# Attention in plain float32, with the second head mixing in two row tiles of TensorE

## The chip, the cores and the metric

The kernel runs on one core of a Trainium2 chip. The metric is the time of one execution on the device in microseconds (us). A core has engines that run side by side, each in its own order: TensorE (PE; its weight loads are listed as PEld), VectorE (DVE), ScalarE (ACT), GpSimd (POOL) and SyncE (SP), which here only issues DMAs. "Granted clock" is the share of TensorE's full 2.4 GHz that the chip gave it; the other level is 1.2 GHz.

## The reference

Attention with two mixings of its twelve heads, and then a mixture of eight experts, each token going to one.

```python
batch, n_heads, seq, head_dim = (8, 12, 448, 64)

scores = scale * np.matmul(q, k.transpose(0, 1, 3, 2))
scores = np.einsum('bhij,hg->bgij', scores, w_pre)          # first mixing of heads
scores = scores - np.max(scores, axis=-1, keepdims=True)
attn = np.exp(scores)
attn = attn / (np.sum(attn, axis=-1, keepdims=True) + 1e-09)
attn = np.einsum('bhij,hg->bgij', attn, w_post)             # second mixing of heads
attn_out = np.matmul(attn, v)
x = attn_out.transpose(0, 2, 1, 3).reshape(B * S, H * D)    # 3584 x 768
...
expert_idx = np.argmax(x @ w_gate, axis=1)                  # E = 8, D = 768, F = 1024
for e in range(E):
    h = np.maximum(x[expert_idx == e] @ w1[e], 0.0)
    out[expert_idx == e] = gate_w * (h @ w2[e])
```

## The kernel before, in words

Each batch has four tiles of queries, three of 120 and one of 88 (`it` 0 to 3; 32 tiles T). For a tile, `qk` computes the scores of one head: the keys and queries are split into a high and a low part in float32r (`ka` and `kb`, `qs`), stacked on the 128 partitions, and two matmuls over 448 keys add up in a PSUM bank `bs`. ScalarE copies it into `si` (queries on partitions, heads and keys along them). `relayout`, a DMA from SBUF to SBUF, turns blocks of 10 queries into `sb`, with the 120 pairs (query, head) on the partitions. `split` makes `sh` and `sl` of it on VectorE. `mix` is the first mixing: three float32r matmuls by the block matrix of `w_pre` (`WH`, `WL`) into a bank `bm`, a maximum on VectorE, the exponential on ScalarE into `et`, with its sum, and `wp`, the block matrix of `w_post` divided by the sums. `post` is the second mixing, which also transposes: for each of four chunks of 112 keys, `et` is the stationary operand (120 rows, 112 columns) and `wp` is streamed (120 columns) into a bank `bp`, which ScalarE copies into `pt`. `av` multiplies by the values `vt`, two heads at once in the two column halves of the array (64 columns each) into `ba`. `rows` turns the result into rows of x with the logits of the gate (`bx`), and `dispatch` sorts the tile's tokens to the experts. All plain float32 matmuls appear in the trace as two instructions each, each with its weight load; a float32r matmul appears as one.

The blocks of all tiles form one sequence of 360 steps u. A table, filled by `at(step, key, function, ...)`, says at which step each function is written, and within a step they are written in the order of their keys; a scheduler then orders each engine's instructions from that, staying close to it. In step u stand the `mix` of block u, the scores of a head of a tile to come (17 steps ahead of it), a relayout 5 steps ahead, a split 2 steps ahead, av of the tile before, and `post` of the block three steps back. The keys of the next batch are loaded and split while the scores of the last tile of a batch (`it == 3`) run, a chunk of two heads at a time through two buffers `kraw`; `vt` has one buffer, loaded after the last `av` of a batch. Behind the attention comes the stage of the experts (`turn_x`, `hidden`, `result`), which runs over the eight experts; its first weights (`load_w`) are loaded in the last steps of the attention.

Of the kernel before, what the change touches and what calls it, by code (L numbers as in the profile page):

```python
# [28 lines left out]
KC = 2                # heads of one chunk of keys  # L29
CAP = 512             # tokens per expert in the straight path  # L30
# [8 lines left out]
def attn_moe_kernel(ctx, tc, qT, kT, v, w_pre, w_post, w_gate, w1, w2, out):  # L39
# [5 lines left out]
    XD = dram.tile([NT, HD], F32, name="XD")          # rows of x by token  # L45
    TB = dram.tile([ROWS, 2], F32, name="TB")         # token id (int32) and gate of each expert's rows

    geom = []
    for T in range(NTILE):
        it = T % 4  # L50
        ni = min(IT, S - it * IT)
        geom.append((T // 4, it, ni, [min(IB, ni - s) for s in range(0, ni, IB)]))

# [1 line left out]
    kq = ctx.enter_context(ExitStack())  # L55
    kraw_p = kq.enter_context(tc.tile_pool(name="kraw", bufs=2, side="right"))
    k_p = kq.enter_context(tc.tile_pool(name="kp", bufs=6, side="right"))
    q_p = kq.enter_context(tc.tile_pool(name="qp", bufs=1, side="right"))
    att = ctx.enter_context(ExitStack())
    v_p = att.enter_context(tc.tile_pool(name="vp", bufs=1))  # L60
    si_p = att.enter_context(tc.tile_pool(name="sip", bufs=2))
    sb_p = att.enter_context(tc.tile_pool(name="sbp", bufs=4))
    sh_p = att.enter_context(tc.tile_pool(name="shp", bufs=3))
    e_p = att.enter_context(tc.tile_pool(name="ep", bufs=5))
    sm_p = att.enter_context(tc.tile_pool(name="smp", bufs=4))
    ps_s = att.enter_context(tc.tile_pool(name="ps_s", bufs=1, space=PSUM))
# [5 lines left out]
    bank_s = [ps_s.tile([P, 512], F32, name=f"bs{n}") for n in range(2)]  # L72
    bank_m = [ps_m.tile([IT, 512], F32, name=f"bm{n}") for n in range(2)]
    bank_p = [ps_p.tile([JC, 512], F32, name=f"bp{n}") for n in range(2)]
    bank_a = ps_a.tile([P, 3, IT], F32, name="ba")
    bank_x = [ps_x.tile([P, 512], F32, name="bx"), bank_s[0]]
    turn = {"s": 0, "m": 0, "p": 0}

    def bank(k, banks):
        turn[k] += 1  # L80
        return banks[turn[k] % len(banks)]

    KK, QQ, VV, SI, SB, SH, EE, PT, XT, KR = ({} for _ in range(10))

    def dma_k(b, c, pool):
        raw = pool.tile([P, KC, S], F32, name="kraw")
        src = kT[b, c * KC:(c + 1) * KC].rearrange("h d j -> d h j")
        for half in range(2):
            nc.sync.dma_start(out=raw[half * D:(half + 1) * D], in_=src)
# [582 lines left out]
```

## Time and profile before

| | us |
|---|---|
| median of 3 runs | 1741.92 |
| lowest and highest run | 1730.40 and 1745.09 |
| profiled execution: span from its first instruction to its last | 1726.5 |
| its own time beside the span | not recorded apart; the runs lie 3.9 to 18.6 above the span, the median 15.4 |

In the profiled execution TensorE is busy for 89% of the span, its weight loads for 78%, VectorE for 61%, ScalarE for 52% and GpSimd for 6%. These are averages over two stages of different kind: the attention, up to about 1150 us, and the experts. The end of a matmul is modelled by the profiler, so the pace of a group is read from its starts, or from its busy time less one instruction's duration.

### The profile page before, as it was taken

What the parts mean: (1) busy time and instruction counts of PE and PEld (TensorE: products, weight loads), DVE (VectorE), ACT (ScalarE), POOL (GpSimd) and SP (SyncE); (2) the same over time, 40 slices, a digit from 0 to 9 for tenths busy, and PEclk for the clock granted to TensorE, in tenths of its full rate; (3) what the DMA queues carried; (4) which work ended last, traced back from release to release, by engine and by line L of the source; (5) the groups of instructions that cost most, each with busy time, mean ns of one, the idle gap of its engine ahead of it and who ended that gap; (6) DMA issues with size and microseconds to landing.
All of it is one profiled execution on the core that took longest, in us unless ns stands there. A gap on an engine that the chain in (4) does not pass through costs nothing. (4 is left out here: it accounts for less than half of the span.)

```text
span 1726.5 us, 30276 instructions
## 1 busy us (share of the span) xinstructions
PE 1541.7 (89%) x11032; PEld 1341.1 (78%) x11032; DVE 1055.8 (61%) x3159; ACT 903.9 (52%) x1940; POOL 109.3 (6%) x119
## 2 busy tenths in 40 slices
PE   5878978987988988998898898968999999999996
PEld 3667867876876877786787787758898988898986
DVE  4677857876877777786786787753433425335330
ACT  4566756765766656675775676633422314224220
POOL 1000000000000000000000000010110201101000
PEclk9999988999999989998998999988999999999998
DMA  8666656666556666665665655634514326145210
GB/s 180 129 134 129 127 117 137 116 134 140 118 126 148 121 137 128 130 126 129 134 117 128 133 110 114 154 70 162 195 67 165 142 78 215 66 153 210 74 62 34
DMA packets 112169, 219.58 MB, mean 127 GB/s; under 512 B 28226, under 2 KB 83538, under 8 KB 112004
## 3 DMA queue, kind: packets, MB, share of 16 engines
q1 hardware_dynamic: 104896, 193.53, 48.3%
q0 software_dynamic: 6064, 23.86, 3.7%
q8 instruction: 98, 1.61, 0.4%
q14 instruction: 67, 0.55, 0.1%
q10 hardware_dynamic: 1044, 0.04, 0.0%
HBM read 118.03 MB, written 23.06 MB: 82 GB/s over the span
## 5 line engine op out<-in xcount | busy, mean ns | idle before, releaser
L256 PE MATMUL bp<-wp,et 120*112 120x120 f32 (+1 forms) x2880 | 386.1, 276 | 4.2 <-ACT pt L258 2.7
L256 PEld LDWEIGHTS bp<-wp,et 120*112 120x112 f32 (+1 forms) x2880 | 346.7, 180 | 45.4 <-issue 21.4
L258 ACT COPY pt<-bp 112x480 f32<-112x480 f32 x360 | 204.3, 568 | 143.1 <-PE bp L256 142.2
L208 ACT COPY si<-bs 120x448 f32<-120x448 f32 (+1 forms) x380 | 200.8, 531 | 140.4 <-PE bs L204 108.0
L271 PE MATMUL ba<-pt,vt 112*64 112x120 f32 (+1 forms) x3072 | 210.7, 276 | 50.1 <-DMA vt<-in_v 40.7
L237 ACT ACTIVATE et<-bm,st 120x448 f32<-120x448 f32 x360 | 229.5, 638 | 43.2 <-DVE st L235 34.9
L271 PEld LDWEIGHTS ba<-pt,vt 112*64 112x64 f32 x3072 | 162.6, 142 | 110.7 <-issue 95.5
L235 DVE TENSOR_REDUCE st<-bm 120x1 f32<-120x448 f32 x360 | 220.9, 614 | 12.4 <-PE bm L233 12.1
L224 DVE TENSOR_TENSOR sl<-sb,sh 120x448 fp32r<-120x448 f32 x360 | 220.5, 615 | 0.3
L223 DVE CAST sh<-sb 120x448 fp32r<-120x448 f32 x360 | 140.0, 389 | 101.6 <-PE bm L232 51.3
L203 PE MATMUL bs<-ka,qs 128*120 128x448 f32 (+1 forms) x384 | 153.7, 400 | 48.0 <-ACT si L208 33.1
L231 PE MATMUL bm<-sh,WH 120*120 120x448 f32 x360 | 167.6, 465 | 7.6 <-DVE sh L223 4.7
L204 PE MATMUL bs<-kb,qs 128*120 128x448 f32 (+1 forms) x384 | 148.5, 387 | 0.6 <-DVE kb L97 0.6
L500 PE MATMUL pm_h<-xh,ah 128*128 128x512 f32 (+1 forms) x384 | 146.9, 383 | 2.2 <-PEq L552 0.8
L500 PE MATMUL pm_h<-xl,ah 128*128 128x512 f32 (+1 forms) x384 | 146.4, 381 | 0.0
L500 PE MATMUL pm_h<-xh,al 128*128 128x512 f32 (+1 forms) x384 | 146.4, 381 | 0.0
L233 PE MATMUL bm<-sl,WH 120*120 120x448 f32 x360 | 137.6, 382 | 0.2 <-DVE sl L224 0.2
L232 PE MATMUL bm<-sh,WL 120*120 120x448 f32 x360 | 137.5, 382 | 0.0
L519 PE MATMUL pm_y<-bh,hh 128*128 128x384 f32 x480 | 127.9, 343 | 0.0
L504 DVE SCALAR_TENSOR_TENSOR hl<-pm_h,hh 128x512 fp32r<-128x512 f32 (+1 forms) x64 | 42.0, 656 | 136.3 <-ACT hh L503 136.3
L203 PEld LDWEIGHTS bs<-ka,qs 128*120 128x120 f32 (+1 forms) x384 | 72.6, 189 | 67.0 <-ACT si L208 39.9
L519 PE MATMUL pm_y<-bl,hh 128*128 128x384 f32 x480 | 123.6, 336 | 0.0
(106 smaller groups left out, 2177.4 us busy)
## 6 DMA issues: line engine op xcount, KB each, us to landing
sb<-si SPq DMA_DIRECT2D x352, 210.0 KB
wraw<-in_w SPq DMA_DIRECT2D x48, 512.0 KB
wraw<-in_w SPq DMA_DIRECT2D x64, 384.0 KB
kraw<-in_kT SPq DMA_DIRECT2D x96, 224.0 KB
qraw<-in_qT SPq DMA_DIRECT2D x48, 360.0 KB
vt<-in_v SPq DMA_DIRECT2D x8, 1344.0 KB
XD<-xr SPq DMA_DIRECT2D x24, 360.0 KB
qraw<-in_qT SPq DMA_DIRECT2D x16, 264.0 KB
```

The costliest lines, as they stand in the source:

```text
L203: nc.tensor.matmul(out=ps[:ni, :S], lhsT=qs, rhs=ka[:, h % KC, :], start=True, stop=False)
L204: nc.tensor.matmul(out=ps[:ni, :S], lhsT=qs, rhs=kb[:, h % KC, :], start=False, stop=True)
L208: nc.scalar.copy(out=SI[T][:ni, h, :], in_=ps[:ni, :S])
L224: nc.vector.tensor_sub(out=sl[:R], in0=sb[:R], in1=sh[:R].bitcast(F32))
L231: nc.tensor.matmul(out=pm[:R, :S], lhsT=WH[:R, :R], rhs=sh[:R], start=True, stop=False)
L235: nc.vector.reduce_max(out=st[:R, 0:1], in_=pm[:R, :S], axis=AX.X, negate=True)
L237: nc.scalar.activation(out=et[:R], in_=pm[:R, :S], func=AF.Exp, bias=st[:R, 0:1], scale=1.0, accum_out=st[:R, 1:2])
L256: nc.tensor.matmul(out=ppv[:, c, :], lhsT=et[:R, c * JC:(c + 1) * JC], rhs=wp[:R, :, :nb], start=True, stop=True)
L258: nc.scalar.copy(out=PT[T][:, :, :, s * IB:s * IB + nb].rearrange("p c h i -> p (c h) i"), in_=pp[:, :NJ * R].rearrange("p (x i) -> p x i" ...
L271: nc.tensor.matmul(out=pa[r * D:(r + 1) * D, :ni], lhsT=VV[b][:, c, h * D:(h + 1) * D], rhs=PT[T][:, c, h, :ni], start=(c == 0), stop=(c = ...
L500: nc.tensor.matmul(out=ph[:, :n], lhsT=wx[:, fs], rhs=xx[:, kt, :n], start=(m == 0), stop=(m == 3 * NK1 - 1))
L519: nc.tensor.matmul(out=py[g][:, :384], lhsT=hx[:, kt, ts], rhs=wx[:, g * 384:(g + 1) * 384], start=(n == 0), stop=(n == 3 * NK2 - 1))
```

## The change

The attention works on plain float32, without high and low parts. `qk` takes a pair of heads: the 64 features of one head lie on partitions 0 to 63, those of the other on 64 to 127, and each head's matmul uses only its row half of the array (64 rows), for 224 keys at a time, each head into its own bank of `bs`; one ScalarE copy takes both. The unit of a step is now 20 queries in two halves of 10 (NB = 2 * IB), 184 units in all. `mix` is one float32 matmul per half, with rows 4 to 123 in use (R0, R1), one maximum over both halves, two exponentials; `wp` is computed by GpSimd. In `post` the rows 4 to 63 hold 5 queries and the rows 64 to 123 the other 5, so that the block matrix has 60 columns (IQ = 5, WPC = 60) and each half of the rows is a matmul of its own, 64 and 60 rows, into its own bank (`bank_p[0]`, `bank_p[1]`); VectorE copies both into `pt`. `bs` and `bm` have a single buffer of two banks each. Keys have buffers for two batches and are loaded while the scores of the second tile (`it == 1`) run, each key once; `vt` has two buffers and is loaded at the eighth unit of the batch before. `post` runs one unit after `mix`, the scores up to 8 units ahead, the relayout 2 units ahead. The opening in which the first tile's scores were ordered by hand is gone.

```diff
+NB = 2 * IB
+IQ = 5
+WPC = H * IQ
+R0, R1 = 4, 124
...
+    bank_s = ps_s.tile([P, 2, 512], F32, name="bs")
+    bank_m = ps_m.tile([P, 2, 512], F32, name="bm")
...
+    def load_k(b, c):
+        kt = k_p.tile([P, S], F32, name="kt")
+        nc.sync.dma_start(out=kt, in_=kT[b, 2 * c:2 * c + 2].rearrange("h d j -> (h d) j"))
+        KK[b, c] = kt
...
+        for n in range(2):
+            ns = slice(n * S // 2, (n + 1) * S // 2)
+            for r in range(2):
+                hs = slice(r * D, (r + 1) * D)
+                nc.tensor.matmul(out=bank_s[:ni, r, ns], lhsT=qt[hs, c, :ni], rhs=kt[hs, ns],
+                                 start=True, stop=True)
+        nc.scalar.copy(out=SI[T][:ni, 2 * c:2 * c + 2, :], in_=bank_s[:ni, :, :S])
+        if it == 1 and b + 1 < B:
+            load_k(b + 1, c)
...
-        nc.tensor.matmul(out=pm[:R, :S], lhsT=WH[:R, :R], rhs=sh[:R], start=True, stop=False)
-        nc.tensor.matmul(out=pm[:R, :S], lhsT=WL[:R, :R], rhs=sh[:R], start=False, stop=False)
-        nc.tensor.matmul(out=pm[:R, :S], lhsT=WH[:R, :R], rhs=sl[:R], start=False, stop=True)
...
+        for c in range(nh):
+            nc.tensor.matmul(out=bank_m[:R1, c, :S], lhsT=Wpre[:R1, :], rhs=sb[:R1, c, :],
+                             start=True, stop=True)
+        nc.vector.reduce_max(out=st[:R1, 0, :nh], in_=bank_m[:R1, :nh, :S], axis=AX.X, negate=True)
+        for c in range(nh):
+            nc.scalar.activation(out=et[:R1, c, :], in_=bank_m[:R1, c, :S], func=AF.Exp,
+                                 bias=st[:R1, 0, c:c + 1], scale=1.0,
+                                 accum_out=st[:R1, 1, c:c + 1])
...
+        wp = e_p.tile([P, 2, WPC], F32, name="wp")
+        for c in range(nh):
+            nc.gpsimd.tensor_scalar(out=wp[:R1, c, :], in0=Wpost[:R1], scalar1=st[:R1, 2, c:c + 1],
+                                    scalar2=None, op0=ALU.mult)
...
-        for c in range(NJ):
-            nc.tensor.matmul(out=ppv[:, c, :], lhsT=et[:R, c * JC:(c + 1) * JC],
-                             rhs=wp[:R, :, :nb], start=True, stop=True)
-        nc.scalar.copy(out=PT[T][:, :, :, s * IB:s * IB + nb].rearrange("p c h i -> p (c h) i"),
-                       in_=pp[:, :NJ * R].rearrange("p (x i) -> p x i", i=nb))
...
+                for r in range(2):
+                    ps = slice(64 * r, 64 if r == 0 else R1)
+                    x0 = (n * NJ + c) * WPC
+                    nc.tensor.matmul(out=bank_p[r][:, x0:x0 + WPC],
+                                     lhsT=et[ps, n, c * JC:(c + 1) * JC],
+                                     rhs=wp[ps, n, :], start=True, stop=True)
...
+                nc.vector.tensor_copy(out=dst, in_=pv.rearrange("p n x i -> p x n i"))
...
-        if pr == NPAIR - 1 and it == 3 and b + 1 < B:
-            load_v(b + 1)
...
-    PL, QLEAD, RLEAD, SLEAD = 3, 17, 5, 2
+    PL, QLEAD, RLEAD = 1, 8, 2
...
+        if it == 0 and b + 1 < B:
+            at(u0 + 8, 2, load_v, b + 1)
+        for c in range(NPAIR):
+            at(max(u0 - QLEAD + c * 5 // 6, -1), 3, qk, T, c)
```

On TensorE, in the middle of the attention, a step before (L231 to L233 mixing, L203 and L204 scores, L271 av, L256 post, L289 rows; the numbers behind a row are how many matmuls in a row it stands for):

```order
L289 MATMUL bx<-xg,xt 120x136 x3
L231 MATMUL bm_106<-sh,WH 120x448
L232 MATMUL bm_106<-sh,WL 120x448
L233 MATMUL bm_106<-sl,WH 120x448
L203 MATMUL bs_104<-ka,qs 120x448
L204 MATMUL bs_104<-kb,qs 120x448
L271 MATMUL ba<-pt,vt 64x120 x8
L256 MATMUL bp_109<-wp,et 112x120 x4
```

And a unit after, at the same place (L209 mixing, L185 scores, L263 av, L237 post, L279 rows):

```order
L237 MATMUL bp_110<-wp,et 112x60
L279 MATMUL bx<-xg,xt 120x136 x3
L209 MATMUL bm<-sb_154,Wpre 124x448 x2
L185 MATMUL bs<-kt,qt 120x224 x4
L263 MATMUL ba<-pt,vt 64x120 x16
L237 MATMUL bp_109<-wp,et 112x60
L237 MATMUL bp_110<-wp,et 112x60
```

The order of the parts is the same; a unit holds two halves of the mixing in a row, a pair of heads, av of one or two pairs, and post as sixteen matmuls that change between the two banks.

On ScalarE where the keys of the next batch are loaded, before (L237 exponential, L258 copy of post, L208 copy of scores, L96 and L116 the high parts of keys and queries):

```order
L237 ACTIVATE et,st<-bm_106,st 120x448
L258 COPY pt<-bp_109 112x48x10
L96 CAST ka<-kraw 128x896
L237 ACTIVATE et,st<-bm_107,st 120x448
L208 COPY si<-bs_104 88x448
L116 CAST qs<-qraw 128x1440
```

And after (L213 exponential, L187 copy of scores, L281 copy of x, L311 exponential of the gate):

```order
L213 ACTIVATE et,st<-bm,st 124x448 x2
L187 COPY si<-bs 120x896
L281 COPY xr<-bx 120x384
L311 ACTIVATE ex,sc<-lgs,sc 120x8
L213 ACTIVATE et,st<-bm,st 124x448 x2
L187 COPY si<-bs 120x896
```

The casts that stood between the exponentials, and the copies of post, are gone from this engine.

On SP's queue at a change of batch, before (L215 relayout, L127 values, L296 rows of x, L109 queries, L89 keys):

```order
L215 DMA sb<-si 120x1x448 x4
L127 DMA vt<-in_v 112x4x768
L296 DMA XD<-xr 88x768
L215 DMA sb<-si 120x1x448 x7
L109 DMA qraw<-in_qT 64x1440
L215 DMA sb<-si 120x1x448
```

And after, at the values' place (L200 relayout, L101 values, L286 rows of x, L96 queries, L88 keys):

```order
L200 DMA sb_154<-si 120x1x448 x2
L101 DMA vt<-in_v 112x4x768
L200 DMA sb_151<-si 120x1x448 x2
L286 DMA XD<-xr 88x768
L200 DMA sb_152<-si 120x1x448 x2
L96 DMA qt<-in_qT 64x6x120
L200 DMA sb_153<-si 120x1x448 x2
```

The values are still issued among the relayouts, but these are now the values of the next batch.

## Rows read from the trace of the kernel before

**Rows 1.** Busy time of each engine in three stretches (before the first mixing, from the first to the last mixing, and after it); the columns are the stretch, its length, busy us and instructions of PE, PEld, DVE, ACT and POOL, the granted clock, the DMA engines' busy share, and GB/s.

```profile
0.00:31.90 31.90, 14.30 (x32) 7.96 (x32) 13.72 (x21) 15.31 (x22) 4.71 (x25) 0.93 0.88 197
31.90:1137.20 1105.30, 984.50 (x8051) 837.74 (x8052) 830.99 (x2798) 713.88 (x1640) 31.53 (x30) 0.94 0.61 128
1137.20:1726.50 589.30, 542.88 (x2952) 495.35 (x2950) 211.07 (x342) 174.74 (x279) 73.03 (x64) 0.97 0.35 122
```

**Rows 2.** The same columns, for an undisturbed stretch and two at a change of batch.

```profile
597.00:634.00 37.00, 37.00 (x330) 32.56 (x329) 30.41 (x106) 25.78 (x62) 0.99 (x1) 1.00 0.58 114
634.70:646.30 11.60, 5.09 (x35) 4.19 (x33) 5.13 (x30) 3.42 (x11) 0.63 (x1) 0.67 0.65 195
...
670.40:678.40 8.00, 3.51 (x23) 3.15 (x21) 3.63 (x10) 3.63 (x9) 0.00 (x0) 0.86 0.58 118
```

**Rows 3.** Waits over the whole span: who waited for whom, us in total, times, the longest.

```profile
ACT ka L96 <- DMA kraw<-in_kT: 55.7, 18, 7.0
DVE kb L97 <- ACT ka L96: 53.7, 25, 5.5
...
PE ba L271 <- DMA vt<-in_v: 40.7, 7, 6.8
...
PE bs L203 <- ACT si L208: 33.1, 14, 5.6
PE bx L289 <- DVE xt L275: 28.3, 7, 5.6
```

**Rows 4.** TensorE's instructions in order of time, a step with av at 88 queries and one without: start, busy us, engine, line, operation, tiles, rows and columns of the weights, what is streamed, and count.

```profile
608.13 0.45 PE L231 MATMUL bm<-sh,WH 120*120 120x448 f32 x1
608.41 0.37 PE L232 MATMUL bm<-sh,WL 120*120 120x448 f32 x1
...
609.02 0.37 PE L204 MATMUL bs<-kb,qs 128*120 128x448 f32 x1
609.32 0.83 PE L271 MATMUL ba<-pt,vt 112*64 112x88 f32 x16
610.08 1.07 PE L256 MATMUL bp<-wp,et 120*112 120x120 f32 x8
610.92 0.44 PE L231 MATMUL bm<-sh,WH 120*120 120x448 f32 x1
...
612.02 0.98 PE L256 MATMUL bp<-wp,et 120*112 120x120 f32 x8
612.76 0.45 PE L231 MATMUL bm<-sh,WH 120*120 120x448 f32 x1
```

**Rows 5.** TensorE's groups by line and shape, 597 to 634 us: busy us, mean duration of one instruction in ns, idle before.

```profile
L256 PE MATMUL bp<-wp,et 120*112 120x120 f32 x113 | 15.1, 273 | 0.0
...
L271 PE MATMUL ba<-pt,vt 112*64 112x88 f32 x96 | 5.0, 245 | 0.0
...
L256 PE MATMUL bp<-wp,et 96*112 96x96 f32 x8 | 0.9, 259 | 0.0
L289 PE MATMUL bx<-xg,xt 128*120 128x136 f32 x6 | 0.9, 279 | 0.0
```

**Rows 6.** As rows 4, for a group of rows and a post of 8 queries (96 columns).

```profile
602.80 0.86 PE L289 MATMUL bx<-xg,xt 128*120 128x136 f32 x6
...
604.50 0.93 PE L256 MATMUL bp<-wp,et 96*112 96x96 f32 x8
```

**Rows 7.** DMA issues by tile and size: engine, count, KB each.

```profile
kraw<-in_kT SPq DMA_DIRECT2D x96, 224.0 KB
qraw<-in_qT SPq DMA_DIRECT2D x48, 360.0 KB
vt<-in_v SPq DMA_DIRECT2D x8, 1344.0 KB
```

**Rows 8.** Groups of ScalarE and VectorE over the whole span, from the page: busy us, mean ns, idle before and what ended it.

```profile
L258 ACT COPY pt<-bp 112x480 f32<-112x480 f32 x360 | 204.3, 568 | 143.1 <-PE bp L256 142.2
L208 ACT COPY si<-bs 120x448 f32<-120x448 f32 (+1 forms) x380 | 200.8, 531 | 140.4 <-PE bs L204 108.0
...
L237 ACT ACTIVATE et<-bm,st 120x448 f32<-120x448 f32 x360 | 229.5, 638 | 43.2 <-DVE st L235 34.9
...
L235 DVE TENSOR_REDUCE st<-bm 120x1 f32<-120x448 f32 x360 | 220.9, 614 | 12.4 <-PE bm L233 12.1
```

**Rows 9.** GpSimd's copies of 128 columns, by line: busy us, mean ns.

```profile
L171 POOL COPY xg<-ident 128x128 f32<-128x128 f32 x6 | 1.5, 283 | 0.0
```

**Rows 10.** The last mixing in order of time: its last matmul, the maximum, and two exponentials in a row (in brackets the idle time before, and what ended it).

```profile
1137.69 0.37 PE L233 MATMUL bm<-sl,WH 96*96 96x448 f32 x1
...
1138.10 0.62 DVE L235 TENSOR_REDUCE st<-bm 96x1 f32<-96x448 f32 x1 [0.20 <-PE bm L233]
...
1138.97 0.64 ACT L237 ACTIVATE et<-bm,st 120x448 f32<-120x448 f32 x1
...
1139.59 0.63 ACT L237 ACTIVATE et<-bm,st 96x448 f32<-96x448 f32 x1
```

**Rows 11.** TensorE's first instruction, and its first mixing.

```profile
10.71 0.73 PE L203 MATMUL bs<-ka,qs 128*120 128x448 f32 x1 [10.71 <-ACT ka L96]
...
31.91 0.73 PE L231 MATMUL bm<-sh,WH 120*120 120x448 f32 x1
```

More of the change, by code (lines that the diff above doesn't have):

```diff
@@ L26 @@
 IB = 10
+NB = 2 * IB
+IQ = 5
+WPC = H * IQ
+R0, R1 = 4, 124
 JC, NJ = 112, 4
 NPAIR = H // 2
-KC = 2
 CAP = 512
@@ L77, in attn_moe_kernel @@
[L77 to L87, printed above, removed]
-        for half in range(2):
-            nc.sync.dma_start(out=raw[half * D:(half + 1) * D], in_=src)
-        KR[b, c] = raw
-    def split_k(b, c, eng=None):
-        raw = KR.pop((b, c))
-        ka = k_p.tile([P, KC, S], F32R, name="ka")
-        kb = k_p.tile([P, KC, S], F32R, name="kb")
-        nc.scalar.copy(out=ka, in_=raw)
-        (eng or nc.vector).tensor_sub(out=kb, in0=raw, in1=ka.bitcast(F32))
-        KK[b, c] = (ka, kb)
@@ L121, in load_q @@
-    def load_q(T):
-        dma_q(T)
-        split_q(T)
+    bank_x = [ps_x.tile([P, 512], F32, name="bx"), bank_s[:, 0, :]]
+    KK, QQ, VV, SI, SB, EE, PT, XT = ({} for _ in range(8))
+    def load_k(b, c):
+        kt = k_p.tile([P, S], F32, name="kt")
+        nc.sync.dma_start(out=kt, in_=kT[b, 2 * c:2 * c + 2].rearrange("h d j -> (h d) j"))
+        KK[b, c] = kt
+    def load_q(T):
+        b, it, ni, _ = geom[T]
+        qt = q_p.tile([P, NPAIR, IT], F32, name="qt")
+        src = qT[b, :, H * it * IT:H * (it * IT + ni)].rearrange("d (c t i) -> t d c i", c=NPAIR, t=2)
+        for half in range(2):
+            nc.sync.dma_start(out=qt[half * D:(half + 1) * D, :, :ni], in_=src[half])
+        QQ[T] = qt
@@ L135, in attn_moe_kernel @@
     nc.scalar.activation(out=warm, in_=warm, func=AF.Exp)
-    first = ExitStack()
-    first_p = first.enter_context(tc.tile_pool(name="kfirst", bufs=H // KC))
-    dma_q(0)
-    for c in range(H // KC):
-        dma_k(0, c, first_p)
+    load_q(0)
+    for c in range(NPAIR):
+        load_k(0, c)
     ident = const.tile([P, P], F32, name="ident")
     make_identity(nc, ident)
-    mask = const.tile([IT, IB], F32, name="mask")
+    mask = const.tile([P, IB], F32, name="mask")
     nc.gpsimd.memset(mask, 1.0)
@@ L168, in attn_moe_kernel @@
+    nc.vector.tensor_tensor(out=Wpost, in0=w12[:, 1, :].unsqueeze(2).to_broadcast([P, H, IQ]),
+                            in1=mask5.unsqueeze(1).to_broadcast([P, H, IQ]), op=ALU.mult)
+    Wpost = Wpost.rearrange("p g i -> p (g i)")
+    sbs = [sb_p.tile([P, 2, S], F32, name=f"sb{n}") for n in range(4)]
+    for t in sbs:
+        nc.gpsimd.memset(t, 0.0)
     xg = const.tile([P, NPAIR, XG], F32, name="xg")
@@ L249, in post @@
-        R = nb * H
         if s == 0:
@@ L392, in attn_moe_kernel @@
         at(ua + 5 * w // NPAIR + 2, 9, dispatch, T)
-    with tc.manual_schedule():
-        split_q(0)
-        split_k(0, 0)
-        split_k(0, 1)
-        for c in range(H // KC):
-            if c + 2 < H // KC:
-                split_k(0, c + 2)
-            for h in range(KC * c, KC * c + KC):
-                qk(0, h)
-    first.close()
-    pt_p = att.enter_context(tc.tile_pool(name="ptp", bufs=2))
-    x_p = att.enter_context(tc.tile_pool(name="xp", bufs=1))
     at(0, 2, load_v, 0)
```

154 lines of the change are left out of this document (61 added, 93 removed).

## The prediction

> **What bounds the kernel now.** I read the stretches first. Before the first head mixing lie 31.9 us, the mixing stage takes 1105.3 us, and from the last mixing to the end 589.3 us pass [rows 1]. The change rewrites the first two and leaves the experts alone. In the mixing stage TensorE is busy for 984.5 of 1105.3 us at a granted clock of 0.94, while VectorE has 831 us and ScalarE 714 us. So TensorE is the bound there, but not a clean one. In an undisturbed stretch it has no idle time and a clock of 1.00; where a batch changes, it is busy for 5.09 of 11.6 us (clock 0.67) and 3.51 of 8.0 us [rows 2]. The waits name the causes: 40.7 us for vt (one buffer, asked for when the last batch is done with it), and 33.1 and 28.3 us for ScalarE's and VectorE's copies, which stand in line behind casts and subtractions of keys whose DMA is late (55.7 and 53.7 us) [rows 3].
>
> To price the undisturbed part I went to TensorE's order of time. A step without av, from one L231 to the next, takes 612.76 - 610.92 = 1.84 us; one with av at 88 queries 610.92 - 608.13 = 2.79 us [rows 4]. Paces come from the same rows. float32r with 448 columns: 609.02 - 608.41 for three, 0.203 us each. A float32 matmul shows as two instructions, each with its own weight load. At 120 columns a group of eight takes 0.98 us, less one duration 0.273 [rows 4, 5], over 7: 0.101 us each; at 136 columns (0.86 - 0.279)/5 = 0.116 [rows 5, 6]. That is 0.85 ns per column. At 96 columns it should be 0.082 and is (0.93 - 0.259)/7 = 0.096: there something else sets the pace, and what is left is the load of 112 weight columns. The av group, in two column halves, does 16 instructions of 88 columns in 0.83 us: (0.83 - 0.245)/7 = 0.083 us per pair, where two in a row would need 0.15. So halves of the array do overlap, and their loads with them (this is columns, not rows). The step with av is 0.95 us longer, its 8 pairs are 0.66: 0.29 us for going into and out of the split mode, 0.145 per switch.
>
> Before, by these paces: mixing 1080 x 0.204 = 220, scores 768 x 0.204 = 157, post 2880 x 0.101 = 291, av 162 (below), rows 384 x 0.116 = 45, switches 384 x 0.145 = 56; 931 us. The stage took 1105: 174 us are lost. Idle time is 1105.3 - 984.5 = 121, and a clock of 0.94 means that 12% of the time ran at 1.2 GHz, which costs some 66 [rows 1]; the two explain it.
>
> **The change, part by part, on TensorE.**
> Scores: per pair of heads four float32 matmuls of 224 columns, eight instructions of 224 x 0.85 = 0.190 us. If both row halves run at once, four pairs in a row: 0.76 us; 32 tiles x 6 pairs x 0.76 = 146 us (before 157). The halved contraction buys no time: it pays for float32.
> First mixing: 360 halves x 2 instructions x 448 x 0.85 ns (0.381 us) = 274 us. That is dearer than three float32r passes (220).
> Post: per ten queries four chunks, two row halves, two instructions: 16 instead of 8, with 60 columns. Matmuls at 60 columns would need 0.051 us, but each loads 112 weight columns, 0.096 us [rows 5, 6]. With both halves loading at once 360 x 8 x 0.096 = 276 us (before 291): the row tiles halve the streaming, and the load takes its place. Bounds: 147 us if a load of 64 rows hides entirely (pairs at 0.051), 553 us if the two halves load one after the other. I take 276, since the only split groups in the trace, av's, load in pairs.
> The rows have no load with fewer than 96 rows. The Trainium skill, TensorE: Matmul & The Clock Gate, section LDWEIGHTS (loading the stationary operand), says that a load takes the columns divided by 1.2 GHz, whatever the rows; for 112 columns that gives an estimate of 93 ns, near this trace's 96, and it speaks against the hope in row tiles: with it post would come to about 269 us, and not to 147.
> av is unchanged: 48 pairs per tile, 0.083 us at 88 queries, 0.113 at 120 (by columns): 24 x 48 x 0.113 + 8 x 48 x 0.083 = 162 us. Rows: 45 us.
> Switches: mixing uses the whole array, scores and post row halves, av column halves. A unit of 20 queries with all four has four switches where two steps had two on average; over a tile's six units I count 21, some 650 in all: 94 us at 0.145. Between zero and twice that: 0 to 188.
> The rows show this cost for column halves only. The Trainium skill, TensorEngine Tiling (Array Packing), Key Properties, says that any change of tiling mode drains the engine; if instead only column mode cost, the total would fall by some 39 us.
> Sum: 146 + 274 + 276 + 162 + 45 + 94 = 997 us of work for the stage, 66 us **more** than before; 5.4 us for each of the 184 units.
>
> **What goes away.** The losses. Keys lose cast and subtraction and land as they are, in twelve buffers, asked for a tile of queries earlier; vt has two buffers and is asked for at the eighth unit of the batch before. The second copy of every key (half of kraw's 96 x 224 KB, 10.75 MB) goes, and that of the queries [rows 7]. SP issues the loads of vt and keys between relayouts as before; vt's 1344 KB delay the relayouts behind it, which have two units (11 us) of lead by the order and more since SP runs ahead. Of the 174 us lost I keep 25 (estimate: start of the clock, a few waits); bounds 0 to 80. Stage 997 + 25 = 1022.
>
> **Other engines, per unit of 5.4 us.** VectorE: one maximum over 896 columns, 2 x 0.614 less one fixed part, about 1.1 us; two copies of 480 elements, priced as ScalarE's 0.568 each; small operations. Some 3 us with dispatch. ScalarE: two exponentials of 0.638 and one copy of 896 columns, less than 2 x 0.531: 2.3 us [rows 8]. Nothing there becomes the bound. wp moves to GpSimd, two operations of 60 columns; 128 columns took 0.283 us there [rows 9], so up to 0.6 us per unit, hidden: post of a unit stands a whole unit later. The new serial loop: bank_m has one buffer, so the next mixing waits for both exponentials, and behind it in TensorE's order stand that unit's scores, av and the post of the unit before, which could run. The loop is: mixing 1.52, hand-over 0.20, maximum 1.1, hand-over 0.25, exponentials 1.25, and back 0.2 [rows 8, 10]: 4.5 us. It hides under the 5.4 us of TensorE, whose lightest units (no av) are near 4.8; it costs 0 as long as TensorE's other work in the unit exceeds 3.0 us.
>
> **Start.** Before, scores begin at 10.71 us and mixing at 31.91 [rows 11]. Half the bytes and no casts come earlier, but bank_s is one buffer, so nine pairs of heads (six, and three of the next tile by the order) go through matmul, hand-over and copy at 2.0 to 2.7 us: I take 27 us (22 to 32). The tail stays 589.3: its last products, dispatch and experts are the same code.
> Span 27 + 1022 + 589.3 = 1638 us. The profiled span before is 1726.5 and the median 1741.92, 15.4 above; with that **1654, say 1655 us**, 5% faster.
>
> **The rivals.**
> *Loads of the two row halves go one after the other.* Place: post. Price 2880 x 0.096 = 276 us: 1931 us, slower. It decides once the second load adds over 87/2880 = 30 ns. For it: no row shows two row halves; against it: column halves load in pairs. 0.11.
> *The row halves do not run at once*, so the change does not do what it says: scores +146 us, post about the same (32 x 0.051 against 16 x 0.096): 1801 us, slower. 0.06.
> *The load of 64 rows hides*: post 147, 129 us less: 1526 us; the loop of 4.5 us then nearly binds at 4.7 per unit. For it only that the 96-column pace has one group of rows behind it. 0.07.
> *The serial loop binds*: VectorE's dispatch operations and copies stand ahead of the maximum in its order; at 5.8 us per unit it would cost 64 us: 1719 us. 0.08.
> Forecast as summed, 1590 to 1725: 0.68.
>
> **How the numbers follow.** About 1% is what a measurement of this kernel can tell from no change (1724 to 1759). Faster: nearly all of 0.68, 0.07, and half of the loop's 0.08: 0.76. Same: the rest of these, 0.05. Slower: 0.17 of the two first rivals and a little for waits I do not see: 0.19. The range reaches from halfway to the hidden loads, 1570, to just short of the halves that do not overlap, 1790; it leaves out the first two rivals and half of the third, and takes in switches at up to twice their price.
>
> **What would show it.** Pairs of scores instructions starting together and 0.19 us apart; post in pairs at 0.096 to 0.10 us (0.05: hidden load; 0.19: serial loads); units of 5.4 us with TensorE never idle; the disturbed steps at batch changes gone and the clock near 1.00 in the stage; mixing instructions 0.38 us apart. It is wrong if units are over 5.8 us, or if TensorE waits for ScalarE's exponentials in most units.

## The result and the profile after

| | before | after |
|---|---|---|
| median (lowest to highest), us | 1739.24 (1730.40 to 1745.09), 4 runs | 1668.19 (1665.59 to 1676.81), 4 runs |
| profiled execution: time, span | -, 1726.5 | 1669.89, 1668.1 |

The ratio is 0.9592 (95% interval 0.9547 to 0.9637): 71 us or 4.1% faster.

The three stretches of the changed kernel, cut as in [rows 1] at its first and last mixing (31.2 and 1070.0 us); the same columns.

```profile
0.00:31.20 31.20, 16.58 (x72) 10.28 (x72) 1.07 (x8) 8.74 (x10) 7.86 (x29) 1.00 0.91 226
31.20:1070.00 1038.80, 1005.17 (x11283) 734.57 (x11282) 563.31 (x1490) 435.68 (x1029) 184.01 (x389) 0.99 0.56 114
1070.00:1668.10 598.10, 548.81 (x2968) 498.62 (x2966) 212.65 (x339) 172.79 (x274) 73.93 (x65) 0.96 0.35 121
```

Between the two profiled executions all of the gain is in the middle stretch, 66.5 us. (That of the kernel before was a quick one: with the 1.8 us that a time lies above its span it took 1728.3 us, less than any of its timed runs.) TensorE does not work less there: it is busy for 1005 us where it was 984. What is gone is idle time (33.6 us in place of 120.8) and low clock (0.99 in place of 0.94). VectorE lost a third of its work and ScalarE four tenths; neither was the bound, at 831 and 714 of 1105 us, and no run shows whether that relief bought anything by itself.

TensorE's waits over the whole span (us, times, longest); the lines that answer to [rows 3].

```profile
PE bs L185 <- ACT si L187: 29.6, 38, 2.9
...
PE bm L209 <- ACT et L213: 10.1, 6, 5.0
```

The waits for vt and xt have left the list. TensorE in order of time, two units in the undisturbed part, the columns of [rows 4]:

```profile
565.39 1.77 PE L209 MATMUL bm<-sb,Wpre 124*124 124x448 f32 x4
567.08 0.83 PE L263 MATMUL ba<-pt,vt 112*64 112x88 f32 x16
567.84 1.78 PE L237 MATMUL bp<-wp,et 64*112 64x60 f32 x32
569.56 0.93 PE L279 MATMUL bx<-xg,xt 128*88 128x136 f32 x6
570.32 1.67 PE L209 MATMUL bm<-sb,Wpre 124*124 124x448 f32 x4
571.92 1.02 PE L185 MATMUL bs<-kt,qt 64*120 64x224 f32 x8
572.87 0.83 PE L263 MATMUL ba<-pt,vt 112*64 112x88 f32 x16
573.63 1.39 PE L237 MATMUL bp<-wp,et 64*112 64x60 f32 x22
575.47 1.02 PE L185 MATMUL bs<-kt,qt 64*120 64x224 f32 x8 [0.46 <-ACT si L187]
576.33 0.71 PE L237 MATMUL bp<-wp,et 64*112 64x60 f32 x10
```

From start to start: mixing takes 1.60 to 1.69 us, scores 0.95, av of 88 queries 0.76, post 1.72, rows 0.76. Post's 32 instructions are 16 pairs, one in each row half: (1.78 - 0.26)/15 = 0.101 us per pair on average; by the starts the first step takes 0.14 us and each later one 0.098. The second unit holds two pairs of heads of scores; the second one finds the bank still with ScalarE, waits 0.46 us, and the scheduler has cut post in two around it. Such a unit takes 6.6 us, the lightest whole ones 4.3 to 4.5; an undisturbed batch of 23 units takes 129.0, or 5.6 each.

### The profile page after: what moved, and what is told of

Read it like the earlier page. It is cut to its first block, busy times and chain, and to the rows that moved or that the text cites. A ratio compares the mean times of both kernels' runs of the same rounds, so it can differ in the third digit from the quotient of the medians.

```text
span 1668.1 us, 35171 instructions
## 1 busy us (share of the span) xinstructions
PE 1570.6 (94%) x14320; PEld 1243.5 (75%) x14320; DVE 777.0 (47%) x1836; ACT 617.2 (37%) x1312; POOL 265.8 (16%) x483
## 5 line engine op out<-in xcount | busy, mean ns | idle before, releaser
L213 ACT ACTIVATE et<-bm,st 124x448 f32<-124x448 f32 x360 | 225.2, 630 | 481.7 <-DVE st L211 338.8
L209 PE MATMUL bm<-sb,Wpre 124*124 124x448 f32 x720 | 319.4, 565 | 11.8 <-ACT et L213 10.1
L237 PEld LDWEIGHTS bp<-wp,et 64*112 64x112 f32 (+1 forms) x5760 | 310.7, 175 | 23.5 <-issue 17.4
L237 PE MATMUL bp<-wp,et 64*112 64x60 f32 (+1 forms) x5760 | 327.2, 260 | 0.3 <-POOL wp L221 0.3
L245 DVE COPY pt<-bp 112x480 f32<-112x480 f32 x352 | 216.3, 651 | 149.0 <-PE bp L237 148.8
L221 POOL TENSOR_SCALAR wp<-Wpost,st 124x60 f32<-124x60 f32 x360 | 153.3, 440 | 774.5 <-DVE st L218 708.6
L211 DVE TENSOR_REDUCE st<-bm 124x2 f32<-124x896 f32 (+1 forms) x184 | 196.9, 1070 | 114.5 <-PE bm L209 104.3
L185 PEld LDWEIGHTS bs<-kt,qt 64*120 64x120 f32 (+1 forms) x1536 | 127.0, 179 | 151.8 <-issue 99.0
L185 PE MATMUL bs<-kt,qt 64*120 64x224 f32 (+1 forms) x1536 | 203.8, 385 | 36.2 <-ACT si L187 29.6
L187 ACT COPY si<-bs 120x896 f32<-120x896 f32 (+1 forms) x192 | 172.9, 901 | 60.3 <-PE bs L185 52.2
L263 PEld LDWEIGHTS ba<-pt,vt 112*64 112x64 f32 x3072 | 148.8, 137 | 55.1 <-issue 37.9
L209 PEld LDWEIGHTS bm<-sb,Wpre 124*124 124x124 f32 x720 | 121.7, 189 | 90.5 <-issue 65.9
L263 PE MATMUL ba<-pt,vt 112*64 112x120 f32 (+1 forms) x3072 | 180.9, 265 | 0.8 <-DVE pt L249 0.4
```

Of the source, the lines that this page charges most:

```text
L185: nc.tensor.matmul(out=bank_s[:ni, r, ns], lhsT=qt[hs, c, :ni], rhs=kt[hs, ns], start=True, stop=True)
L187: nc.scalar.copy(out=SI[T][:ni, 2 * c:2 * c + 2, :], in_=bank_s[:ni, :, :S])
L209: nc.tensor.matmul(out=bank_m[:R1, c, :S], lhsT=Wpre[:R1, :], rhs=sb[:R1, c, :], start=True, stop=True)
L211: nc.vector.reduce_max(out=st[:R1, 0, :nh], in_=bank_m[:R1, :nh, :S], axis=AX.X, negate=True)
L213: nc.scalar.activation(out=et[:R1, c, :], in_=bank_m[:R1, c, :S], func=AF.Exp, bias=st[:R1, 0, c:c + 1], scale=1.0, accum_out=st[:R1, 1, c ...
L221: nc.gpsimd.tensor_scalar(out=wp[:R1, c, :], in0=Wpost[:R1], scalar1=st[:R1, 2, c:c + 1], scalar2=None, op0=ALU.mult)
```

## The experiments

Times are medians and ratios to the kernel before, measured beside it on the same chip. Because the experts' stretch, whose code is the same everywhere, took between 586.6 and 602.3 us in the profiled executions of these kernels (`post_56` aside), a difference of less than some 10 us is read from the middle stretch or not at all. The middle stretch itself scatters: it took 1038.8 us in the changed kernel and 1045.6 and 1046.0 us in `k_spread` and `spread`, whose matmuls are the same. The changed kernel was not run again beside the others, so a difference to it is one between separate measurements; the medians of the kernel before lie between 1739 and 1745 us in them.

**Where the gain comes from: the values' second buffer.** `after_v1` undoes it, `after_vk1` undoes the keys' second set too; `before_v` gives the kernel before an early load of the values and nothing else, `before_kv` also earlier keys.

```diff
 after_v1
-        if it == 0 and b + 1 < B:
-            at(u0 + 8, 2, load_v, b + 1)
-        vt = v_p[b % 2].tile([JC, NJ, HD], F32, name="vt")
+        vt = v_p[1].tile([JC, NJ, HD], F32, name="vt")
 in av
+        if pr == NPAIR - 1 and it == 3 and b + 1 < B:
+            load_v(b + 1)
 after_vk1: this, and
-    k_p = kq.enter_context(tc.tile_pool(name="kp", bufs=2 * NPAIR, side="right"))
+    k_p = kq.enter_context(tc.tile_pool(name="kp", bufs=NPAIR, side="right"))
-        if it == 1 and b + 1 < B:
+        if it == 3 and b + 1 < B:
             load_k(b + 1, c)
```

> The changed kernel with one part undone: the values have one buffer again and are asked for when the last value products of a batch are done. Theory (what the change gains are the stalls at the changes of batch, of which vt was the longest, 40.7 us of TensorE's waiting in the kernel before, and the clock falls behind each): 7 changes of batch at 5 to 8 us, 35 to 55 us back, 1703 to 1723 us. Rival (in the new order the next batch's mixings and scores cover the load): 1664 to 1680 us.

Measured: 1724.68 us (1722.99 to 1727.70), ratio 0.9898 (0.9860 to 0.9936): 56.5 us above the changed kernel, just past the upper end of the theory. Its middle stretch, the wait, TensorE at one change of batch, and the row of the 3.4 us behind the wait:

```profile
29.50:1124.70 1095.20, 1035.76 (x11290) 757.06 (x11288) 562.34 (x1490) 436.05 (x1029) 184.03 (x389) 0.96 0.54 110
...
PE ba L263 <- DMA vt<-in_v: 31.3, 7, 5.9
...
205.83 3.36 PE L263 MATMUL ba<-pt,vt 112*64 112x120 f32 x32 [4.90 <-DMA vt<-in_v]
209.12 1.90 PE L237 MATMUL bp<-wp,et 64*112 64x60 f32 x32
...
206.00:209.40 3.40, 3.40 (x36) 3.10 (x33) 0.00 (x0) 0.00 (x0) 0.00 (x0) 0.50 0.21 69
```

The stretch is 56.4 us longer for 31.3 us of waiting. Idle time grew by 25.8 us (some other waits shrank); the rest is in the busy time, 1035.8 against 1005.2 us for the same instructions, at a granted clock of 0.96 against 0.99. After the 4.90 us of idleness the clock is at 0.50, its lower level, and the 32 instructions of av start over 3.29 us, where two groups of 16 with 120 queries take 2 x 0.97 elsewhere. A stall cost almost twice its own length.

> The changed kernel with both loads undone: values as in the kernel before, and six buffers of keys, each asked for again when the last tile of a batch has used it. Theory (the whole gain is in these loads): 1715 to 1745 us, the time of the kernel before. Rival (the keys, which are no longer cast, have some five units or 28 us until the next batch's scores want them, and only the values stall): like the run with the values alone, within 10 us.

Measured: 1720.76 us (1716.84 to 1724.18), ratio 0.9866 (0.9825 to 0.9907); vt 27.9 us in 7 waits, the only wait for keys the one at the start. The time lies in both ranges, but it is not above that of `after_v1`: with the values in one buffer the keys' second set buys nothing, as the rival had it. Whether it buys something beside values in two buffers is not shown, since here the stall for vt gives the keys time as well; no run undoes the keys alone.

```diff
 before_v
-        vt = v_p.tile([JC, NJ, HD], F32, name="vt")
+        vt = v_p.tile([JC, NJ, HD // 2], F32, name=f"vt{half}")
+        hs = slice(half * HD // 2, (half + 1) * HD // 2)
...
-        if pr == NPAIR - 1 and it == 3 and b + 1 < B:
-            load_v(b + 1)
+        if pr % 3 == 2 and it == 3 and b + 1 < B:
+            load_v(b + 1, pr // 3)
 before_kv: this, and in qk
+        if it == 2 and b + 1 < B and h in (H - 3, H - 1):
+            dma_k(b + 1, (h - (H - 3)) // 2, kraw_p)
...
-            load_k(b + 1, h // KC)
+            split_k(b + 1, h // KC)
+            if h // KC + 2 < H // KC:
+                dma_k(b + 1, h // KC + 2, kraw_p)
```

> The kernel before with the values in two half tiles by heads, each asked for as soon as its heads are done, and the keys as they were. Theory (vt is the first cause at the change of batch: its 40.7 us and half of the 28.3 us in which TensorE waits for xt go): 1690 to 1705 us. Rival (behind vt stands the chain of kraw, cast, subtraction and scores, 55.7 and 53.7 us, which is as long): 1725 to 1745 us.

Measured: 1691.36 us (1684.35 to 1693.92), ratio 0.9690 (0.9647 to 0.9734), in the theory's range. From the other side, then: 51 of the 71 us, by the medians, are had by loading the values earlier in the kernel before, with its hi/lo splits, its order and its post unchanged. Between the profiled executions it is less: the middle stretch is 33 us shorter than before (1072.5 against 1105.3), where that of the changed kernel is 66.5 shorter. The wait for vt is gone from its list; these head it now, and below them its middle stretch:

```profile
PE bs L204 <- ACT si L209: 34.2, 14, 4.9
PE bx L290 <- DVE xt L276: 23.1, 6, 5.8
PE bm L232 <- ACT et L238: 20.0, 13, 4.4
...
31.40:1103.90 1072.50, 973.53 (x8055) 827.33 (x8055) 830.80 (x2800) 710.96 (x1640) 32.02 (x30) 0.95 0.63 132
```

The theory's sum came about in another way than it said: of the 28.3 us for xt 23.1 are left, and the waits for the exponentials, 1.6 us in the kernel before, have grown to 20.0.

> The kernel before, with nothing but its loads moved: the values in two half tiles by heads, each reloaded as soon as its half of av is done with it, and each chunk of keys asked for two chunks (four steps) before its cast. Theory (the change won by losing the waits at the changes of batch, 174 us of lost time, while its work on TensorE grew by 66 us): the waits go here too, 100 to 150 us, 1590 to 1640 us, faster than the changed kernel. Rival (the float32 attention is itself what is faster): 1700 us or more.

Measured: 1684.21 us (1677.65 to 1690.64), ratio 0.9651 (0.9603 to 0.9699). The earlier keys add 7 us, less than the intervals tell apart (13 us between the profiled middle stretches, 1059.6 and 1072.5); the theory of 1590 to 1640 failed.

```profile
ACT ka L96 <- DMA kraw<-in_kT: 13.1, 10, 3.2
...
PE bs L204 <- ACT si L209: 34.8, 13, 5.4
...
PE bx L294 <- DVE xt L280: 5.3, 6, 1.5
```

With the waits for kraw (56.6 us in `before_v`) those for xt went, 23.1 to 5.3. Those for si and et (19.9 us) stayed, and those for pt grew from 12.8 to 23.7 us: late keys are not their main cause.

**What the kernel before loses beyond that.** `before_kvg` takes the casts out of the way:

```diff
 before_kv, and in split_k
-        nc.scalar.copy(out=ka, in_=raw)
+        if b:
+            nc.gpsimd.tensor_copy(out=ka, in_=raw)
+            eng = nc.gpsimd
+        else:
+            nc.scalar.copy(out=ka, in_=raw)
         (eng or nc.vector).tensor_sub(out=kb, in0=raw, in1=ka.bitcast(F32))
```

> The kernel before with the values in two half tiles and the keys asked for early (that measured 1684 us), and now the high part and the subtraction of the keys made by GpSimd, which is idle, and no longer by ScalarE and VectorE; the split itself stays. Theory (what the kernel before still loses with the loads mended is the line behind these casts on ScalarE and VectorE, where TensorE waits 34.8 us for the copies of scores and 23.7 us for pt): 1655 to 1672 us, the time of the changed kernel. Rival (the lateness is that of the DMAs and relayouts on SyncE's queue, or GpSimd is slower at it and the next batch's scores wait for it): 1680 us or more.

Measured: 1709.04 us (1705.61 to 1722.30), ratio 0.9800 (0.9764 to 0.9835): slower than `before_kv`. GpSimd's two groups, and then the place where a step of the next batch takes 10.7 us, by TensorE, SyncE's queue and ScalarE:

```profile
L101 POOL TENSOR_TENSOR kb<-kraw,ka 128x896 fp32r<-128x896 f32 x42 | 94.7, 2256 | 3.4
L97 POOL CAST ka<-kraw 128x896 fp32r<-128x896 f32 x42 | 40.6, 966 | 234.7 <-PE bs L208 217.2 <-DMA kraw<-in_kT 10.6 <-PE bs L209 3.0
...
270.93 0.73 PE L208 MATMUL bs<-ka,qs 128*120 128x448 f32 x1 [4.19 <-ACT si L213]
...
258.88 6.31 SPq L224 DMA_DIRECT2D sb<-si  x4
265.29 3.48 SPq L89 DMA_DIRECT2D kraw<-in_kT  x2
...
270.35 0.96 ACT L213 COPY si<-bs 120x448 f32<-120x448 f32 x2 [3.81 <-DMA kraw<-in_kT]
```

ScalarE has no cast in its line here and TensorE still waits 4.19 us for its copy of scores, and the copy waits 3.81 us for a DMA. The page names kraw, which this copy does not read; what it writes is the buffer si, from which the relayouts read that SyncE issues, four of them, from 258.88 to 265.19 us. That these are what it waits for is argued, since the profile does not show when they land. So at this place TensorE waits for a transfer and not for a cast. The kernel tells no more than that: the subtraction takes 2.26 us on GpSimd and 1.09 on VectorE, and GpSimd's own slowness is mixed into the total. Which part of the remaining 16 to 23 us (21 to 34 by the middle stretches) between `before_kv` or `before_v` and the changed kernel belongs to the smaller key traffic, which to the larger units or to the engines' smaller work, stays open.

**Post, the part that the change is named for.** `post_whole` gives it the whole array again, with everything else as changed; `post_serial` runs the two row halves one after the other; `post_56` loads only half the columns, and so leaves out half of the second mixing.

```diff
 post_whole
-WPC = H * IQ
+WPC = H * IB
...
-                for r in range(2):
-                    nc.tensor.matmul(out=bank_p[r][:, x0:x0 + WPC], lhsT=et[ps, n, c * JC:(c + 1) * JC],
-                                     rhs=wp[ps, n, :], start=True, stop=True)
+                nc.tensor.matmul(out=bank_p[n][:, c * WPC:(c + 1) * WPC],
+                                 lhsT=et[:R1, n, c * JC:(c + 1) * JC],
+                                 rhs=wp[:R1, n, :], start=True, stop=True)
 post_serial: loops in the order r, n, c in place of n, c, r
 post_56
-                                     lhsT=et[ps, n, c * JC:(c + 1) * JC],
+                                     lhsT=et[ps, n, c * JC:c * JC + JC // 2],
```

> The changed kernel with post on the whole array again: 124 rows, 120 streamed columns, one matmul per chunk of keys; all else as changed. My theory (the load of 112 weight columns sets the pace of post, 0.099 us per pair of instructions, so that row tiles buy nothing): eight instructions of 0.102 us per ten queries in place of eight pairs of 0.099, some 9 us more over the stage, and one switch of mode per unit fewer (184 x 0.145 = 27 us): 1668 - 18 = 1650 us. Rival (the streaming sets the pace, and row tiles halve it): post takes twice as long, 285 us more, about 1950 us. Second rival (GpSimd's wp of 120 columns or VectorE's copies come onto the path): 1668 or above.

Measured: 1659.72 us (1659.63 to 1665.57), ratio 0.9523 (0.9481 to 0.9564). TensorE:

```profile
568.15 1.89 PE L231 MATMUL bp<-wp,et 124*112 124x120 f32 x16
569.88 0.86 PE L266 MATMUL bx<-xg,xt 128*88 128x136 f32 x6
```

1.73 us from post to rows, where the row tiles took 1.72. The row tiling of post neither gains nor loses anything that these runs can tell: the middle stretch is 1033.4 us in place of 1038.8, and the intervals of the two ratios overlap. The theory's 18 us did not come: TensorE's busy time in the stretch fell by 2.5 us.

> The changed kernel with the matmuls of post written half by half: all of the upper rows first, then all of the lower rows, so that neighbours use the same row half. Theory (two row halves load and stream at once only when they alternate): each instruction then waits for its own load, 0.098 us, 16 per ten queries in place of 8 pairs of 0.099: 285 us more, 1950 us. Rival (TensorE overlaps loads within a row half as well, or the halves do not overlap in the changed kernel either): 1668 us.

Measured: 1884.01 us, one run: 216 us above the changed kernel, the theory's sign and three quarters of its size.

```profile
566.82 3.01 PE L236 MATMUL bp<-wp,et 64*112 64x60 f32 x32
569.76 0.96 PE L278 MATMUL bx<-xg,xt 128*120 128x136 f32 x6
```

The same 32 instructions take 2.94 us in place of 1.72, (3.01 - 0.26)/31 = 0.089 us each on average. By their starts they follow each other at 0.098 us within a half, which is the theory's pace; at the seam the last four of the upper half run beside the first four of the lower one, which is why the size came out smaller. Loads of the two halves overlap where the halves alternate, or meet.

> The changed kernel with 56 instead of 112 weight columns per matmul of post; the other half of each chunk of keys is left out, so the second mixing is half done. Theory (the load sets the pace): pairs go from 0.099 to 0.053 us, 132 us less; units then come near the serial loop of mixing, maximum and exponentials (4.5 us), which keeps some of it: 1540 to 1570 us. Rival (a cost per instruction in row mode sets the pace): pairs stay at 0.09 to 0.10, 1668 us.

Measured: 1660.32 us, one run. A pair now takes (1.05 - 0.22)/15 = 0.055 us, so the load of the stationary columns is what post's pace is made of. The time did not follow. A unit with little work stops at 4.43 us, where TensorE waits for the exponentials. The larger loss comes once in a batch, in six of them: TensorE waits up to 7.84 us for a copy of scores, and that copy for a relayout (sb<-si):

```profile
269.63 1.75 PE L211 MATMUL bm<-sb,Wpre 124*124 124x448 f32 x4
...
274.06 1.77 PE L211 MATMUL bm<-sb,Wpre 124*124 124x448 f32 x4 [0.73 <-ACT et L215]
...
245.02 0.91 ACT L189 COPY si<-bs 120x896 f32<-120x896 f32 x1 [6.83 <-DMA sb<-si]
245.98 1.85 PE L187 MATMUL bs<-kt,qt 64*120 64x224 f32 x8 [7.84 <-ACT si L189]
...
PE bs L187 <- ACT si L189: 71.5, 38, 7.8
PE bm L211 <- ACT et L215: 24.8, 26, 7.0
30.40:1021.90 991.50, 901.20 (x11282) 605.75 (x11281) 556.59 (x1489) 434.58 (x1028) 183.41 (x388) 0.97 0.59 120
```

TensorE was relieved of 104 us (1005.2 to 901.2) and the stretch fell by 47: the rest went into waits for the copies of scores (L189; 71.5 us where the changed kernel has 29.6) and for the exponentials (L215; 24.8 and 10.1). The total does not show even that, since with half of the second mixing missing the tokens go to other experts, whose stretch took 636.5 us. The theory was right on the pace and wrong on the time.

**Ways to make the changed kernel faster.**

```diff
 post_early
-            at(u0 + s + PL, 7, post, T, s)
+            at(u0 + s + PL, 3.5, post, T, s)
 k_spread
-        if it == 1 and b + 1 < B:
+        if it in (1, 2) and c % 2 == it - 1 and b + 1 < B:
             load_k(b + 1, c)
 spread
-            at(max(u0 - QLEAD + c * 5 // 6, -1), 3, qk, T, c)
+            at(max(u0 - QLEAD + c, -1), 3, qk, T, c)
 whole_both: post_whole with k_spread and spread
```

> The changed kernel (1668 us) with one number altered: the second mixing of the unit before is written right behind the first mixing, ahead of the value products, so that a unit runs first mixing, scores, second mixing, value products and TensorE changes between the full-height mixing and scores and the products once less. Theory (each change of row shape costs TensorE 0.09 to 0.15 us in this stage, as the gaps at mixing to scores and second to first mixing showed, and the stage is TensorE's own work): 184 units x 0.09 to 0.15 us = 17 to 27 us less, 1641 to 1651 us. Rival (the changes lie beside waits, or the second mixing now waits for the weights that GpSimd scales): 1665 us or more.

Measured: 1661.10 us (1654.73 to 1666.44), ratio 0.9524 (0.9477 to 0.9572). The middle stretch:

```profile
30.70:1058.00 1027.30, 993.02 (x11284) 743.71 (x11282) 553.16 (x1490) 435.66 (x1029) 182.66 (x389) 0.99 0.57 115
```

11.5 us less, all of it busy time of TensorE; the total lies between the theory and its rival. The theory counted 184 changes of mode removed (whole array for mixing and rows, row halves for scores and post, column halves for av). In the order of the trace the stretch has 573 of them in place of 630, only 57 fewer: a unit without av or without scores has none to lose, and a second pair of scores, which waits for its bank, now falls into the middle of av and adds two. So one change is worth about 0.2 us, above the theory's 0.09 to 0.15. A unit with one group of each part says the same, 5.32 us from mixing to mixing in the changed kernel and 5.13 here:

```profile
593.17 1.75 PE L209 MATMUL bm<-sb,Wpre 124*124 124x448 f32 x4
594.85 1.02 PE L185 MATMUL bs<-kt,qt 64*120 64x224 f32 x8
595.80 1.04 PE L263 MATMUL ba<-pt,vt 112*64 112x120 f32 x16
596.77 1.78 PE L237 MATMUL bp<-wp,et 64*112 64x60 f32 x32
598.49 1.77 PE L209 MATMUL bm<-sb,Wpre 124*124 124x448 f32 x4
...
589.03 1.75 PE L209 MATMUL bm<-sb,Wpre 124*124 124x448 f32 x4
590.71 1.02 PE L185 MATMUL bs<-kt,qt 64*120 64x224 f32 x8
591.56 1.70 PE L237 MATMUL bp<-wp,et 64*112 64x60 f32 x32
593.19 1.04 PE L263 MATMUL ba<-pt,vt 112*64 112x120 f32 x16
594.16 1.77 PE L209 MATMUL bm<-sb,Wpre 124*124 124x448 f32 x4
```

(A rule of the Trainium skill, TensorEngine Tiling (Array Packing), Key Properties, that a change of tiling mode drains the engine, agrees in sign; the number is this run's.) The waits for si grew from 29.6 to 34.1 us.

> The changed kernel with the next batch's six key loads issued over two query tiles, every other one, in place of all six in one tile. Theory (the unit of 7.7 us in each batch, where the copy of the scores waits for the relayouts and TensorE for that copy, 29.6 us of TensorE's waiting in 38 places, comes from SyncE's queue, on which six loads at 2.4 us of issue delay the relayouts): 10 to 20 us less, 1648 to 1658 us. Rival (the relayouts are late for another reason, or the waits only move): 1665 to 1670 us.

Measured: 1676.35 us (1671.28 to 1685.03), ratio 0.9614 (0.9561 to 0.9666): no gain, as the rival had it, though the time lies above its range. Its batches take 128 to 133 us (the changed kernel's 129 to 134) and the wait is unchanged:

```profile
PE bs L185 <- ACT si L187: 29.8, 37, 3.5
```

My theory on the unit of 7.7 us was wrong. Its TensorE rows hold two pairs of scores, av and rows, and 0.44 us of waiting: it is long because it has much to do.

> The changed kernel with one pair of heads of the next tile's scores in every unit, where before the six pairs went into five units, two of them in one. Theory (the stage is TensorE's own work, which stays the same to the instruction): 1664 to 1672 us. Rival (the units with two pairs make the copies of the scores queue up and TensorE wait for them, and even units take the 29.6 us of these waits away): 1640 to 1650 us.

Measured: 1666.80 us (1657.57 to 1673.14), ratio 0.9529 (0.9480 to 0.9578). 23 waits for si in place of 38, still 26.6 us of them, a batch 127 to 135 us: as the theory had it, the work sets the pace, not how it is spread over the units.

> The changed kernel with the second mixing on all rows at once (that alone measured 1660 us), the key loads over two tiles and one pair of heads in every unit. Theory (the waits for the copies of the scores go, about 20 us of them, with the work of TensorE unchanged): 1638 to 1650 us, faster than both kernels. Rival (the pace is that of TensorE's work and of the loop through the mixing, the waits only stand where slack is): 1656 to 1664 us.

Measured: 1655.69 us (1652.45 to 1656.27), ratio 0.9477 (0.9437 to 0.9517). It is the lowest time of all, faster than the kernel before and, by intervals that do not touch, than the changed one; but its middle stretch is 1036.4 us against 1038.8, and its profiled execution gains mainly in the experts' stretch (589.1 against 598.1), whose code is the same. That the edits make it faster is therefore not shown; that they cost nothing is. The theory of 1638 to 1650 us failed.

## Why the prediction was right, and where its terms were off

Forecast 1655 us, measured 1668; the sign and the main reason hold: more work for TensorE, and a loss of 174 us of which 34 us of idle time are left. The experiments give the reason its size from both sides: undoing the values' load alone gives back 56.5 of 71 us, doing it alone in the kernel before brings 51 by the medians and 33 of 66.5 by the profiled stretches. That the number came within 13 us is in part luck, as the last point below says.

The terms for the middle stretch, measured as starts in TensorE's order times their counts (176 whole units and 8 half ones, 192 pairs of heads):

| term | forecast, us | measured, us |
|---|---|---|
| first mixing | 274 | 176 x 1.69 + 8 x 0.85 = 304 |
| scores | 146 | 192 x 0.94 = 180 |
| post | 276 | 176 x 1.72 + 8 x 0.86 = 310 |
| av | 162 | 144 x 0.97 + 48 x 0.76 = 176 |
| rows | 45 | 64 x 0.77 = 49 |
| changes of mode, apart | 94 | in the rows above |
| work | 997 | 1019 |
| losses kept | 25 | 33.6 of idle time |

The counts are those of the whole attention, as in the forecast. Some 20 us of the 1019 lie outside the stretch: nine pairs of scores before its start, and behind its end the last mixing, three halves of post, seven pairs of av and three groups of rows. The 1000 us within, 3 us of the dispatch's small matmuls and the idle time make 1037 of its 1038.8 us.

*Pace of post.* Right, and the choice between the bounds (147, 276, 553) is the step that carried the most: pairs at 0.101 us where 0.096 to 0.10 was said. `post_56` shows the load as its cause and `post_serial` shows what the rival of loads one after the other would have looked like; the order of the loops decides between the two.

*Changes of mode.* Mis-sized: 1019 - 903 (the forecast without switches) = 116 us against 94, some 7 us of it post's pairs, which follow at 0.098 us in place of 0.096. The stretch has 630 changes where 650 were counted, so one costs 0.17 to 0.18 us on average and not 0.145; those that `post_early` took out were worth about 0.2.

*What goes away.* Right in sum, loose in its parts. I put vt, the casts and the chain of keys side by side; the values' buffer alone is worth over 50 us, and the second set of keys showed no gain. That the copies stand behind the casts of late keys held for xt and not for si: in `before_kv` xt's wait fell to 5.3 us and si's stayed at 34.8. I priced the stalls by idle time and clock apart, and `after_v1` shows both following one cause.

*The serial loop.* 4.5 us, as worked out: units of `post_56` with less work than that wait for the exponentials and take 4.43. The rival of the hidden load was priced at 1526 us with the loop "nearly" binding; by `post_56` that was too low. There 57 of the 104 us of which TensorE was relieved did not come off the stretch: 15 us are longer waits for the exponentials, 42 longer waits for the copies of scores, which the prediction had not priced.

*VectorE and GpSimd.* The maximum took 1.09 us (1.1 said), VectorE's copy of post 0.651 (0.568 priced from ScalarE), wp 0.88 us per unit on GpSimd (up to 0.6 said); all hidden, as forecast.

*Start and end.* 31.2 us in place of 27: nine pairs of heads at 2.86 us each, above the 2.0 to 2.7 that I allowed. Their matmuls ran at about half their later pace (1.85 us in place of 1.02), as [rows 11] already showed: 0.73 us for an instruction that takes 0.37 to 0.45 in [rows 4]. The experts' stretch took 598.1 in place of 589.3, within what it varies between executions. And the step that hid these: I added 15.4 us for what lies around the span. The time of a run lies 1.8 us above its own span (1669.89 and 1668.1); the 15.4 was the distance of a quick profiled run from the median. Start, stage and end were 4, 17 and 9 us too low, and that term 13.6 too high. The stage's 1022 us also count what lies outside the stretch, some 17 us at the forecast's paces, which the start's 27 us and the end's 589.3 us hold once more; within the stretch its terms were some 34 us too low. That two errors of the other sign made up for most of this was luck.

## What to carry to other kernels

Where a profile has an undisturbed part without idle time and a stage that is longer than its pace times its steps, look first for the one transfer that can only start when the last user of its buffer is done: here the second buffer of 1344 KB carries 56 of the 71 us when it is undone, and an early load alone gave the old kernel 51 by the medians. What the rewritten arithmetic around it brought was not separated. A wait of TensorE should be priced with the slower clock behind it, almost twice its length here. And before splitting the rows of a matmul that streams few columns, see whether its pace is that of streaming or of loading the stationary columns; if it is the load, row halves ran here at best even with the whole array, and only when they alternated.

## What the runs showed of the hardware that was not expected

- Two row halves load and multiply at once when they alternate: pairs with 112-column loads start 0.098 us apart. When sixteen of one half follow each other, each single one starts 0.098 us behind the last; yet in `post_serial` the first of the lower half starts 6 ns after the thirteenth of the upper one, before the upper half is through. Whether the engine or the order of its instructions brings that about is not shown.
- Averages over a group hide its slow first step. Pairs in alternating halves ran at 0.055 us on average with loads of 56 columns and at 0.101 with 112, by their later starts at 0.053 and 0.098; with 112 columns on the whole array and 120 streamed it is (1.89 - 0.27)/15 = 0.108 us on average and 0.102 by the later starts.
- In the opening the eight instructions of a pair of heads took 1.85 us where they take 1.02 later, with 1.00 us of waiting between the pairs, and the first mixing took 3.28 us from start to start in place of 1.69. The row of that stretch gives a granted clock of 1.00, but the clock entries kept in the trace begin only at 34.8 us, with full speed, and the row counts time without an entry as full. It is no measurement of the opening. The pace there fits the lower level, and it ends where the entries begin:

```profile
9.44 1.85 PE L185 MATMUL bs<-kt,qt 64*120 64x224 f32 x8 [1.00 <-ACT si L187]
...
31.21 3.35 PE L209 MATMUL bm<-sb,Wpre 124*124 124x448 f32 x4
34.49 1.16 PE L185 MATMUL bs<-kt,qt 64*120 64x224 f32 x8
```

- GpSimd took 2.26 us for a subtraction of 128 x 896 elements and VectorE 1.09, while the cast of the same size took GpSimd 0.97 and ScalarE 0.94.
